# Row factors in fewer operations, three scale products moved to ScalarE, and a longer planned lag for eight spread matmuls

## The chip, the cores and the metric

The kernel runs on one core of a Trainium2 chip. The metric is device time in microseconds (us) for one launch, the median of several runs; lower is better. Engines are named as the profile names them: PE (TensorE matmul), PEld (TensorE weight load, which overlaps PE), DVE (VectorE), ACT (ScalarE), POOL (GpSimd), SP (SyncE, which here only issues DMAs). An engine with a small q behind it (SPq, POOLq) is that engine's queue issuing something.

## The reference

Three stages follow one another. Sizes: 2 batches, 8 heads, 768 steps, head size 40; so 1536 tokens of width 320.

```
# 1. gated linear attention, step by step (here done in chunks of 128 steps)
m_new = max(f + m, i);  f_stab = exp(f + m - m_new);  i_stab = exp(i - m_new)
C = f_stab * C + i_stab * outer(v, k);  n = f_stab * n + i_stab * k
y = sigmoid(o) * (C q) / max(|n.q|, 1)
# 2. dense mixture of 4 experts, every token through every expert
out = sum_e p[:, e] * (relu(x @ w1[e]) @ w2[e])        # w1: 320x1024, w2: 1024x320
# 3. routed mixture of 8 experts, capacity 384 tokens each
e = argmax(x @ w_gate);  y = gate * (relu(x @ w1[e]) @ w2[e])
```

The result is [1536, 320] in 32-bit floats.

## The kernel before

**Precision by splitting.** Matmuls run on 16-bit floats, and each 32-bit operand is split into a high and a low 16-bit part. Before a split, an operand is scaled by a power of two taken from its largest absolute value; `pow2_scale` makes that scale and its inverse with a few tiny DVE operations on exponent bits (lines 437 to 455). The inverses are multiplied back in later.

**Attention.** The 1536 tokens are 12 units (2 batches of 6 chunks of 128 steps), one tile of 128 tokens each. `front(u)` loads a unit, forms scales, decay and scores; `back(u)` applies the running state, updates it, forms the output row `y`, its scale `xs` and inverse `invx[:, u]`, splits it (`split_rows`) and transposes it by DMA into `xT`. Units 0 to 3 (`FP`) work in 32 bits and need no scales. Units 4 to 11 have four scales in `sm[:, 12:16]` and four inverses `iv` in `sm[:, 16:20]` (of q, k, v and the state). From them `front` forms three products on DVE: `iv1*iv2` (line 998), `iv1*iv2*iv0` (line 1000) and `iv0*iv3` (line 1004); the third scales the chunk decay `qd` on ACT (line 1008). They are read in `back`: `qd` by line 1224, the second by lines 1250 and 1255, the first by the state update of line 1291. Lines 1022 and 1028 split q and k, and line 1034 transposes them by DMA for the score matmuls of line 1114.

**Dense experts.** Weights are numbered k = 0 to 3 for the dense experts, 4 to 11 for the routed ones. Experts 0 and 1 run tile by tile between the attention units (`tile_ops`): layer 1 in two halves (PE line 645 into a PSUM bank, evacuated by ACT line 664 and DVE line 666), layer 2 (PE line 657), and then the accumulation `acc[t] += po * cf` on DVE (line 698; ACT line 692 for the first expert of a tile). The row factor `cf = pw[t, k] * invx[t]` is one number per token; line 686 forms it on POOL, one operation for each of 12 tiles and 4 experts, 48 in all. Experts 2 and 3 run afterwards over groups of four tiles (`group_ops`), and each tile that expert 3 finishes is routed at once (`route`).

**Weight preparation.** `w_max` finds a weight's largest magnitudes per partition (ACT line 528 or DVE line 533), reduces them over partitions on POOL into one `row` value (line 546), and spreads it over 128 partitions with a one-column PE matmul, the *spread* (line 552). The DVE operations of `pow2_scale` (lines 441 to 453) follow, then `w_conv` makes the high part (ACT line 590) and the low part (DVE line 595). Each of the two layers' weights passes through one raw buffer (`wraw`), in the order 0, 1, 2, 3, 8, 9, 10, 11, 4, 5, 6, 7: the next load (SP line 423) waits until the conversion before has read the buffer. Weights 8 to 11 are also stored to DRAM and fetched again later (`w_store`, `w_fetch`, line 503); after the last weight, 7, is converted, the copy of weight 8 is fetched into the raw buffers themselves, where layer 1 of an early window reads it.

**What sets the order.** Nothing issues in source order. `Sched` collects every operation with its engine, a cost in us, its reads and writes, then plays the whole program through (`starts`) and emits each engine's instructions in the planned order. `urgency` gives each operation a latest start, working back along the PE order given by the `at` keys; the most urgent ready one goes first. Spreads are different: `spot` puts a spread and the operation behind it into `now`, so PE takes a spread as soon as its planned ready time comes, ahead of all else; its key in `SPREAD_AT` only shapes the urgency of what leads to it. In planned time a spread in `late` becomes ready `SLACK` = 1.0 us after each operation it waits for (line 192). The last argument of `spot` (line 555) decides that: true for weights 1 to 3 and 8 to 11, false for 0 and 4 to 7. Engines execute their queues in order, so an instruction whose input is later than planned holds what is queued behind it. PE also gets filler matmuls (line 417) in planned gaps at the start.

Of the kernel before, what the change touches and what calls it, by code (L numbers as in the profile page):

```python
# [24 lines left out]
NT = B * NC  # L25
# [44 lines left out]
class Sched:  # L70
# [9 lines left out]
    def __init__(self):  # L80
        self.ops, self.last, self.readers, self.ahead = [], {}, {}, 0.0
        self.used, self.warm, self.filled = {}, None, 0.0
        self.spots, self.now, self.late, self.bank_of = [], set(), set(), {}

    def add(self, eng, us, fn, r=(), w=(), at=0.0):
        i = len(self.ops)
# [19 lines left out]
    def spot(self, fn, view, r, w, at, us):  # L106
        i = len(self.ops)
        self.add("PE", 0.07, lambda: fn(view(self.bank_of[i])), r, w, at)
        self.spots.append(i)
        self.now |= {i, i + 1}  # L110
        if us:
            self.late.add(i)
        return lambda: view(self.bank_of[i])

    @staticmethod
# [41 lines left out]
    def starts(self, lst):  # L157
        ops = self.ops
        n = len(ops)
        unit = [{"SCAT": "POOL", "TURN": "DMA", "ADMA": "ACT"}.get(op[0], op[0]) for op in ops]  # L160
        left = [len(op[3]) for op in ops]
        est, start = [0.0] * n, [0.0] * n
        users = [[] for _ in range(n)]
        free, ready, pipe, lanes, count = {}, {}, 0.0, [], 0
        for i, op in enumerate(ops):
            for d in op[3]:
                users[d].append(i)
            free[unit[i]] = self.BEGIN.get(unit[i], 0.0)
            if not left[i]:
                ready.setdefault(unit[i], []).append(i)  # L170
        while count < n:
            t, e = min((max(free[e], min(est[i] for i in c)), e) for e, c in ready.items() if c)
            i = min((i for i in ready[e] if est[i] <= t + self.HOLD[e]), key=lambda i: (i not in self.now, lst[i], i))
            ready[e].remove(i)
            if e == "DMA" and len(lanes) >= 8 and t < lanes[-8]:
                free[e] = lanes[-8]
                ready[e].append(i)
                continue
            start[i] = max(t, est[i])
            us = ops[i][1]  # L180
            count += 1
            free[e] = end = start[i] + us
            if e == "DMA":
                if ops[i][0] == "DMA":
                    free[e] = start[i] + 0.43
                    us = us if us >= 0.8 else 0.15
                    end = pipe = max(pipe, free[e]) + us
                else:
                    end = pipe = max(pipe, end)
                lanes.append(end + 1.7)  # L190
            for q in users[i]:
                est[q] = max(est[q], end + self.lag(ops[i][0], ops[q][0]) + self.care(ops[i][0], ops[q][0], end) + (SLACK if q in self.late else 0.0))
# [58 lines left out]
def xlstm_moe_kernel(ctx: ExitStack, tc: tile.TileContext, a, cap: int):  # L251
# [243 lines left out]
    def w_fetch(k, m, r=(), when=None, us=2.0):  # L495
# [17 lines left out]
    SPREAD_AT = {  # L513
        0: (SEQ["L", 0, 0] - 1.02, SEQ["M", 0, 0] - 2.02), 1: (SEQ["L", 1, 0] - 1.02, SEQ["M", 1, 0] - 1.02),
        2: (len(SEQ) - 0.1, at3 - 9.935), 3: (at3 - 5.61, at3 + 0.065), 8: (at3 + 0.39, at3 + 0.405),
        9: (at3 + 2.01, at3 + 2.03), 10: (at3 + 2.065, at3 + 2.095), 11: (at3 + 2.305, at3 + 2.39),
        4: (at3 + 4.005, at3 + 4.012), 5: (at3 + 4.054, at3 + 4.065), 6: (at3 + 4.19, at3 + 4.205), 7: (at3 + 4.405, at3 + 4.415),
    }

    def w_max(k, m):  # L520
        raw = wraw[m - 1].rearrange("p c f -> p (c f)")
        ks, n = ("wsm", k, m), 6 if m == 1 else 4
        w = raw.shape[1] // n
        am, t, mx = wsm[:, k, m - 1, 0:n], wsm[:, k, m - 1, 7:8], wsm[:, k, m - 1, 10:11]
        sc, iv = wscale(k, m)

        def part(i):
            nc.scalar.activation(  # L528
                out=junk[:, 0:w], in_=raw[:, i * w:(i + 1) * w], func=AF.Abs, accum_out=am[:, i:i + 1]
            )  # L530
# [23 lines left out]
        mx = sch.spot(  # L554
            spread, lambda b: bank[b][:, col:col + 1], [(ks, "row"), "const"], [(ks, "m")], SPREAD_AT[k][m - 1], 0 < k < 4 or k > 7
        )
        pow2_scale(sc, iv, t, mx, (CW1, CW2)[m - 1], [(ks, "m")], (ks, "i"), ks)
        if m == 2:
            vec(
                0.07, lambda: nc.vector.tensor_tensor(invp[:, k:k + 1], wscale(k, 1)[1], iv, ALU.mult),  # L560
                [(ks, "i"), (("wsm", k, 1), "i")], [("invp", k)],
            )
            if k < E1:
                vec(
                    0.13,
                    lambda: nc.vector.tensor_scalar(pw[:, :, k], probs[:, :, k], invp[:, k:k + 1], None, ALU.mult),
                    [("invp", k), "probs"], [("pw", k)],
                )
# [98 lines left out]
            [kp, kh] + ex, [kl],  # L667
        )

    begun = set()  # L670

    def l2_ops(k, t, wb, hh, hl, j, keys, at, extra=()):
        kp = ps_tile("o")
        po = bank[kp]
        for half in range(2):
# [262 lines left out]
    def front(u):  # L938
# [7 lines left out]
        pv2, qd = sm[:, 20:22], sm[:, 24:32]  # L946
        kr, kpb = ("raw", i3), ("pb", i3)
        va = raw[:, VA0:VA0 + HD]
        kr2 = ("raw2", i3)
# [37 lines left out]
        if not fp:  # L987
# [10 lines left out]
            vec(0.11, lambda: nc.vector.tensor_scalar(pv2[:, 0:1], iv1, iv2, None, ALU.mult), [("iv", u)], [("pv", u)])  # L998
            vec(
                0.09, lambda: nc.vector.tensor_scalar(pv2[:, 1:2], iv1, iv2, iv[:, 0:1], ALU.mult, ALU.mult),  # L1000
                [("iv", u)], [("pvq", u)],
            )
            vec(
                0.09, lambda: nc.vector.tensor_scalar(sm[:, 22:23], iv[:, 0:1], iv[:, 3:4], None, ALU.mult),
                [("iv", u)], [("iv03", u)],
            )
            act(
                0.22, lambda: nc.scalar.activation(out=qd, in_=qd3[:, b, c], func=AF.Copy, scale=sm[:, 22:23]),
                [("iv03", u), "qdec"], [("qd", u)],
            )  # L1010

# [167 lines left out]
    def back(u):  # L1179
# [4 lines left out]
        CC = Chr[i2]  # L1184
        kh, kl, kw = kdr[i2]
        sm = usm[:, u]
        pv2, qd, den = sm[:, 20:22], sm[:, 24:32], sm[:, 32:40]
# [56 lines left out]
        if fp and c > 0:  # L1244
            vec(0.45, lambda: nc.vector.tensor_tensor(O, pi, O, ALU.add), ["x2", ("O", i2)], [("O", i2)])
        elif fp:
            O, kO = pi, "x2"
        elif c > 0:
            vec(
                0.45, lambda: nc.vector.scalar_tensor_tensor(O, pi, pv2[:, 1:2], O, ALU.mult, ALU.add),  # L1250
                ["x2", ("O", i2), ("pvq", u)], [("O", i2)],
            )
        else:
            vec(
                0.45, lambda: nc.vector.tensor_scalar(O, pi, pv2[:, 1:2], None, ALU.mult),
                ["x2", ("pvq", u)], [("O", i2)],
            )
        if c < NC - 1:
# [27 lines left out]
            if fp:  # L1286
                vec(0.48, c_add, ["x3", kC], [kC])
            else:
                vec(
                    0.45,  # L1290
                    lambda: nc.vector.scalar_tensor_tensor(Cb, px[0:D], pv2[0:D, 0:1], Cb, ALU.mult, ALU.add),
                    ["x3", kC, ("pv", u)], [kC],
                )
            if fp and u + 1 not in FP:
# [727 lines left out]
```

## Time and profile before

| what | value |
|---|---|
| median of 3 runs | 496.33 us (495.67 to 498.98) |
| the profiled execution | 497.3 us, of which the span is 495.6 |
| PE busy | 477.2 us, 96% of the span |
| DVE, ACT, POOL busy | 338.7, 312.3, 131.6 us |
| PE's own waits | 11.2 us in 14 entries, longest 2.8 (at the start) |
| TensorE's granted clock | 0.989 of full speed over the span |

The profile comes from one execution of the program. The span runs from the first instruction to the last; the time of a run is a little longer. Busy shares are averages over stages with different limits, so each stage is read by itself. Where a line belongs to a helper (`pow2_scale`, `split_rows`, `evac_ops`), many operations share it, and the tile names tell them apart.

### The profile page before, as it was taken

The numbers are of one execution on the slowest core, as the hardware profiler recorded it, in microseconds if no ns is written. First come the engines' busy times: TensorE is split into PE (matmuls) and PEld (weight loads), VectorE is DVE, ScalarE is ACT, GpSimd is POOL, SyncE is SP. The second block draws the span as 40 slices with busy tenths as digits, with TensorE's granted clock in tenths as the row PEclk, the third lists the DMA queues.
The fourth block names the chain that finished last, engine by engine and source line by source line (L and its number), as shares of the span: only waits on it lengthen the run. The fifth ranks groups of instructions, "written<-read, shape, count | busy, mean of one in ns | idle before, by whom it ended". The sixth has DMA issues, their size and how long they took to land. (4 is left out here: it accounts for less than half of the span.)

```text
span 495.6 us, 13700 instructions
## 1 busy us (share of the span) xinstructions
PE 477.2 (96%) x5482; PEld 367.8 (74%) x5482; DVE 338.7 (68%) x971; ACT 312.3 (63%) x666; POOL 131.6 (27%) x243
## 2 busy tenths in 40 slices
PE   7999999999989899999999999999999999999994
PEld 6998989868878798887564746565565798878883
DVE  4599998799999834653968594879899882212120
ACT  1699989567687854956765668779789450322220
POOL 4533243665875410200010010000404011311111
PEclk9799999999999999999999999999999999999998
DMA  7879594264533795808695967727284536999300
GB/s 225 274 241 231 149 282 68 76 146 102 104 60 67 203 345 200 237 16 293 200 300 201 345 239 277 232 82 208 83 227 78 166 147 86 302 193 300 140 27 25
DMA packets 70772, 88.90 MB, mean 179 GB/s; under 512 B 48641, under 2 KB 56307, under 8 KB 70702
## 3 DMA queue, kind: packets, MB, share of 16 engines
q1 hardware_dynamic: 69502, 84.23, 59.9%
q0 software_dynamic: 1200, 3.73, 2.3%
q8 instruction: 45, 0.74, 0.6%
q14 instruction: 25, 0.20, 0.1%
HBM read 55.89 MB, written 21.70 MB: 157 GB/s over the span
## 5 line engine op out<-in xcount | busy, mean ns | idle before, releaser
L657 PEld LDWEIGHTS <-arena 128*128 128x128 f16 (+1 forms) x1416 | 136.1, 98 | 53.6 <-issue 2.5
L645 PEld LDWEIGHTS <-w 128*128 128x128 f16 x1792 | 97.0, 98 | 4.3 <-issue 2.8
L645 PE MATMUL ph<-xT,w 128*128 128x128 f16 (+3 forms) x1664 | 96.1, 218 | 1.2 <-DVE usm L443 0.9
L645 PEld LDWEIGHTS <-arena 128*128 128x128 f16 x960 | 64.2, 98 | 42.9 <-issue 1.5
L657 PE MATMUL po<-w,arena 128*128 128x320 f16 (+1 forms) x600 | 86.2, 299 | 1.3 <-DVE acc L698 1.3
L528 ACT ACTIVATE junk<-raw 128x512 bf16<-128x512 f32 (+1 forms) x105 | 69.5, 662 | 9.8 <-DMA raw<-in_moe_w_dram 8.2
L657 PE MATMUL po<-arena 128*128 128x320 f16 x504 | 71.3, 299 | 0.4 <-ACT arena L590 0.4
L666 DVE SCALAR_TENSOR_TENSOR arena<-ph,arena 128x512 f16<-128x512 f32 x80 | 54.5, 683 | 21.5 <-ACT arena L664 21.2
L645 PE MATMUL ph<-xT,arena 128*128 128x512 f16 (+4 forms) x512 | 66.7, 284 | 0.2 <-DMA xT<-disp 0.2
L590 ACT ACTIVATE w<-raw,wsm 128x640 f16<-128x640 f32 (+1 forms) x56 | 51.0, 959 | 18.2 <-DVE wsm L448 18.1
L664 ACT ACTIVATE arena<-ph 128x512 f16<-128x512 f32 x80 | 47.0, 587 | 24.2 <-PE ph L645 14.1
L595 DVE SCALAR_TENSOR_TENSOR w<-raw,wsm,w 128x640 f16<-128x640 f32 (+1 forms) x56 | 57.4, 1049 | 3.1 <-ACT w L590 3.0
L645 PE MATMUL x<-xT,arena 128*128 128x128 f16 (+4 forms) x448 | 52.2, 270 | 0.0
L546 POOL CROSS_LANE_REDUCE wsm<-wsm 128x1 f32<-128x6 f32 (+1 forms) x24 | 10.0, 418 | 103.0 <-ACT junk L528 71.1
L657 PE MATMUL x<-arena 128*128 128x320 f16 (+1 forms) x240 | 34.6, 300 | 0.4 <-ACT arena L1754 0.4
L595 DVE SCALAR_TENSOR_TENSOR arena<-raw,wsm,arena 128x640 f16<-128x640 f32 (+1 forms) x28 | 30.4, 1101 | 2.3 <-ACT arena L590 2.3
L590 ACT ACTIVATE arena<-raw,wsm 128x640 f16<-128x640 f32 (+1 forms) x28 | 25.5, 954 | 3.6 <-DVE wsm L448 3.6
L686 POOL TENSOR_TENSOR cfs<-pw,invx 128x1 f32<-128x1 f32 x48 | 17.0, 386 | 37.1 <-DVE invx L453 31.9
L698 DVE SCALAR_TENSOR_TENSOR acc<-po,cfs,acc 128x320 f32<-128x320 f32 x30 | 16.4, 546 | 14.6 <-PE po L657 7.5
L1765 POOL DMA_INDIRECT out_dram<-acc,usm x13 | 12.6, 973 | 46.1 <-ACT acc L1762 39.0
L1175 POOL TENSOR_TENSOR arena<-arena 128x512 f16<-128x512 f32 x16 | 20.6, 1305 | 12.6 <-ACT arena L1171 12.6
L1759 DVE SCALAR_TENSOR_TENSOR arena<-x,arena 128x512 f16<-128x512 f32 (+1 forms) x10 | 6.5, 652 | 24.4 <-ACT arena L1754 24.4
(235 smaller groups left out, 658.5 us busy)
## 6 DMA issues: line engine op xcount, KB each, us to landing
raw<-in_moe_w_dram SPq DMA_DIRECT2D x36, 512.0 KB
raw<-in_moe_w_dram SPq DMA_DIRECT2D x24, 640.0 KB
ws<-w SPq DMA_DIRECT2D x8, 768.0 KB
ws<-w SPq DMA_DIRECT2D x8, 640.0 KB
arena<-in_att_dram SPq DMA_DIRECT2D x8, 492.0 KB
disp<-zero SPq DMA_DIRECT2D x1, 3936.0 KB
arena<-ws SPq DMA_DIRECT2D x4, 768.0 KB
arena<-ws SPq DMA_DIRECT2D x4, 640.0 KB
```

Of the source, the lines that this page charges most:

```text
L528: nc.scalar.activation(out=junk[:, 0:w], in_=raw[:, i * w:(i + 1) * w], func=AF.Abs, accum_out=am[:, i:i + 1])
L546: 0.7 if k == 0 else 1.0, lambda: nc.gpsimd.tensor_reduce(row, am, AX.XYZWC, ALU.max), parts + ["wz"],
L590: lambda sl=sl: nc.scalar.activation(out=wh[:, sl], in_=raw[:, sl], func=AF.Copy, scale=sc),
L595: lambda sl=sl: nc.vector.scalar_tensor_tensor(wl[:, sl], raw[:, sl], sc, wh[:, sl], ALU.mult, ALU.subtract),
L645: nc.tensor.matmul(out=out, lhsT=wb[wi][:, c, f * 128:(f + 1) * 128], rhs=rhs(xc), start=(i == 0), stop=(i == LAST))
L657: nc.tensor.matmul(out=po[0:n, 0:DM], lhsT=hs[:, f, sl], rhs=ws[:, f, :], start=(f == 0 and i == 0), stop=(f == NF - 1 and i == 2),)
L664: act(0.52, lambda: nc.scalar.activation(out=hh, in_=ph, func=AF.Relu), [kp] + ex, [kh])
L666: 0.6, lambda: nc.vector.scalar_tensor_tensor(hl, ph, 0.0, hh, ALU.max, ALU.subtract),
L686: 0.26, lambda: nc.gpsimd.tensor_tensor(cf, pw[:, t, k:k + 1], invx[:, t:t + 1], ALU.mult),
L698: lambda: nc.vector.scalar_tensor_tensor(acc[:, t], po[:, 0:DM], cf, acc[:, t], ALU.mult, ALU.add),
L1175: 1.3, lambda j=j: nc.gpsimd.tensor_tensor(Wl[:, j::2], pb[:, j::2], Wh[:, j::2], ALU.subtract),
L1765: nc.gpsimd.indirect_dma_start(out=view_of(), out_offset=bass.IndirectOffsetOnAxis(ap=ix[0:n], axis=0), in_=acc[0:n, y], in_offset=None, b ...
```

## The change

Four edits. (1) Row factors: experts 2 and 3 get one POOL operation each over all 12 tiles; experts 0 and 1 get, for tiles 4 to 11, one ACT operation per tile that makes both factors; tiles 0 to 3 stay as they were. So 48 POOL operations become 10, and 8 ACT operations are new. (2) The three products per unit leave DVE: ACT makes `iv1*iv2`, and then, in one operation over two neighbouring columns, `iv3*iv0` and `iv1*iv2*iv0`. So 24 DVE operations go and 16 ACT operations come; `qd` now follows two ACT operations. (3) `late` holds a multiple of `SLACK`: 3 for the spreads of weights 8 to 11 (two each), 1 as before for weights 1 to 3. (4) The spread keys of weight 9 move by 0.02, two layer-1 pieces of a group.

```
-            self.late.add(i)
+            self.late[i] = us
...
-  ... + (SLACK if q in self.late else 0.0))
+  ... + (SLACK * self.late.get(q, 0)))
...
-        9: (at3 + 2.01, at3 + 2.03), 10: ...
+        9: (at3 + 2.03, at3 + 2.05), 10: ...
...
-  ... SPREAD_AT[k][m - 1], 0 < k < 4 or k > 7
+  ... SPREAD_AT[k][m - 1], 3 if k > 7 else int(0 < k < 4)
...
-        pool(
-            0.26, lambda: nc.gpsimd.tensor_tensor(cf, pw[:, t, k:k + 1], invx[:, t:t + 1], ALU.mult),
-            [("pw", k), ("xs", t, "inv")], [("cf", t, k)],
-        )
+        if (t, k) not in factored:
+            if k > 1:
+                js, ts, on_act = [k], range(NT), False
+            elif t < 4:
+                js, ts, on_act = [k], [t], False
+            else:
+                js, ts, on_act = [0, 1], [t], True
...
+            if on_act:
+                act(0.2, lambda: nc.scalar.activation(
+                        out=cfs[:, t, 0:2], in_=pw[:, t, 0:2], func=AF.Copy, scale=invx[:, t:t + 1]), r, w)
+            else:
+                tx = slice(ts[0], ts[-1] + 1)
+                pool(0.26, lambda: nc.gpsimd.tensor_tensor(cfs[:, tx, k], pw[:, tx, k], invx[:, tx], ALU.mult), r, w)
...
-            vec(0.11, lambda: nc.vector.tensor_scalar(pv2[:, 0:1], iv1, iv2, None, ALU.mult), ...)
-            vec(0.09, lambda: nc.vector.tensor_scalar(pv2[:, 1:2], iv1, iv2, iv[:, 0:1], ALU.mult, ALU.mult), ...)
-            vec(0.09, lambda: nc.vector.tensor_scalar(sm[:, 22:23], iv[:, 0:1], iv[:, 3:4], None, ALU.mult), ...)
+            act(0.2, lambda: nc.scalar.activation(out=pv, in_=iv1, func=AF.Copy, scale=iv2), [("iv", u)], [("pv", u)])
+            act(0.2, lambda: nc.scalar.activation(out=sm[:, 21:23], in_=sm[:, 19:21], func=AF.Copy, scale=iv[:, 0:1]),
+                [("iv", u), ("pv", u)], [("pvq", u), ("iv03", u)])
             act(
-                0.22, ... activation(out=qd, in_=qd3[:, b, c], func=AF.Copy, scale=sm[:, 22:23]),
+                0.22, ... activation(out=qd, in_=qd3[:, b, c], func=AF.Copy, scale=sm[:, 21:22]),
```

## Rows read from the trace of the kernel before

**Rows 1.** The page: busy time, share of the span and instructions of each engine.
```profile
PE 477.2 (96%) x5482; PEld 367.8 (74%) x5482; DVE 338.7 (68%) x971; ACT 312.3 (63%) x666; POOL 131.6 (27%) x243
```

**Rows 2.** Windows: length, then busy time of each engine, clock, DMA share, GB/s.
```profile
48.00:206.00 158.00, 152.69 (x2213) 131.22 (x2211) 133.22 (x343) 118.61 (x248) 70.43 (x123) 1.00 0.59 155
...
100.00:175.00 75.00, 69.69 (x1045) 58.72 (x1044) 70.16 (x175) 58.12 (x122) 45.49 (x59) 1.00 0.51 115
200.00:300.00 100.00, 99.01 (x769) 64.21 (x767) 70.14 (x130) 66.01 (x126) 8.24 (x22) 1.00 0.70 231
300.00:400.00 100.00, 99.57 (x719) 61.93 (x717) 81.93 (x317) 78.31 (x173) 15.90 (x31) 1.00 0.58 173
398.00:400.00 2.00, 2.00 (x43) 2.00 (x41) 1.45 (x9) 1.64 (x5) 0.00 (x0) 1.00 0.97 397
400.00:402.00 2.00, 2.00 (x43) 2.00 (x41) 1.88 (x18) 1.49 (x6) 0.00 (x0) 1.00 0.09 28
```

**Rows 3.** Waits of PE, by releaser: total, times, longest (us).
```profile
PE ph L417 <- POOL zero L759: 2.8, 1, 2.8
PE x L1114 <- DMA arena<-arena: 1.3, 2, 1.1
PE po L657 <- DVE acc L698: 1.3, 1, 1.3
PE x L1200 <- ACT arena L1171: 1.1, 1, 1.1
PE x L552 <- POOL wsm L546: 1.0, 1, 1.0
PE ph L645 <- DVE usm L443: 0.9, 1, 0.9
...
PE x L1268 <- POOL arena L1152: 0.4, 1, 0.4
```

**Rows 4.** Timeline, DVE around one unit's three products: start, us, instruction.
```profile
141.60 0.20 DVE L1004 TENSOR_SCALAR usm<-usm 128x1 f32<-128x1 f32 x1
141.72 0.27 DVE L1000 TENSOR_SCALAR usm<-usm 128x1 f32<-128x1 f32 x1
141.91 0.20 DVE L998 TENSOR_SCALAR usm<-usm 128x1 f32<-128x1 f32 x1
...
142.03 0.14 DVE L453 TENSOR_SCALAR invx<-usm 128x1 uint32<-128x1 uint32 x1
```

**Rows 5.** One line each: count, ns min/median/max, first and last start.
```profile
L1008 ACT ACTIVATE usm<-arena,usm x8: 292/295/307, 59.7 to 154.7; 128x8 f32<-128x8 f32 x8
L686 POOL TENSOR_TENSOR cfs<-pw,invx x48: 179/190/2827, 51.1 to 205.0; 128x1 f32<-128x1 f32 x48
L657 PE MATMUL po<-arena x504: 296/299/301, 244.9 to 470.4; 128*128 128x320 f16 x168
```

**Rows 6.** Waits of ACT between 48 and 206 us.
```profile
ACT arena L622 <- DVE usm L448: 3.9, 4, 1.8
```

**Rows 7.** Timeline, PE's wait at 118.29 and what DVE did before it.
```profile
117.03 0.54 DVE L1050 SCALAR_TENSOR_TENSOR arena<-arena,usm 128x328 f16<-128x328 f32 x1
...
117.56 0.67 DVE L666 SCALAR_TENSOR_TENSOR arena<-ph,arena 128x512 f16<-128x512 f32 x1
...
118.29 1.95 PE L645 MATMUL ph<-xT,w 128*128 128x128 f16 x32 [0.89 <-DVE usm L443]
```

**Rows 8.** Timeline, two maxima and the spreads behind them.
```profile
208.79 0.32 POOL L546 CROSS_LANE_REDUCE wsm<-wsm 128x1 f32<-128x6 f32 x1 [3.62 <-ACT junk L528]
...
212.53 0.17 PE L552 MATMUL x<-wsm,call 128*128 128x1 bf16 x1
...
288.12 1.30 POOL L546 CROSS_LANE_REDUCE wsm<-wsm 128x1 f32<-128x4 f32 x1 [7.52 <-DVE wsm L533]
...
289.47 0.16 PE L552 MATMUL x<-wsm,call 128*128 128x1 bf16 x1 [0.99 <-POOL wsm L546]
...
292.60 0.15 DVE L441 TENSOR_SCALAR wsm<-x 128x1 f32<-128x1 f32 x1
```

**Rows 9.** Waits of the SP queue between 200 and 402 us.
```profile
SPq L423 <- DVE w L595: 88.2, 24, 14.4
```

**Rows 10.** Timeline, the fetch into the raw buffers and its first reader.
```profile
393.02 1.51 SPq L503 DMA_DIRECT2D raw<-ws  x3
...
400.61 1.56 PE L645 MATMUL ph<-xT,raw 128*128 128x128 f16 x25
```

More of the change, by code (lines that the diff above doesn't have):

```diff
@@ L82, in __init__ @@
         self.used, self.warm, self.filled = {}, None, 0.0
-        self.spots, self.now, self.late, self.bank_of = [], set(), set(), {}
+        self.spots, self.now, self.late, self.bank_of = [], set(), {}, {}
     def add(self, eng, us, fn, r=(), w=(), at=0.0):
@@ L191, in starts @@
             for q in users[i]:
-                est[q] = max(est[q], end + self.lag(ops[i][0], ops[q][0]) + self.care(ops[i][0], ops[q][0], end) + (SLACK if q in self.late else 0.0))
+                est[q] = max(est[q], end + self.lag(ops[i][0], ops[q][0]) + self.care(ops[i][0], ops[q][0], end) + (SLACK * self.late.get(q, 0)))
                 left[q] -= 1
@@ L515, in xlstm_moe_kernel @@
         2: (len(SEQ) - 0.1, at3 - 9.935), 3: (at3 - 5.61, at3 + 0.065), 8: (at3 + 0.39, at3 + 0.405),
-        9: (at3 + 2.01, at3 + 2.03), 10: (at3 + 2.065, at3 + 2.095), 11: (at3 + 2.305, at3 + 2.39),
+        9: (at3 + 2.03, at3 + 2.05), 10: (at3 + 2.065, at3 + 2.095), 11: (at3 + 2.305, at3 + 2.39),
         4: (at3 + 4.005, at3 + 4.012), 5: (at3 + 4.054, at3 + 4.065), 6: (at3 + 4.19, at3 + 4.205), 7: (at3 + 4.405, at3 + 4.415),
@@ L554, in w_max @@
         mx = sch.spot(
-            spread, lambda b: bank[b][:, col:col + 1], [(ks, "row"), "const"], [(ks, "m")], SPREAD_AT[k][m - 1], 0 < k < 4 or k > 7
+            spread, lambda b: bank[b][:, col:col + 1], [(ks, "row"), "const"], [(ks, "m")], SPREAD_AT[k][m - 1], 3 if k > 7 else int(0 < k < 4)
         )
@@ L668, in evac_ops @@
         )
-    begun = set()
+    begun, factored = set(), set()
     def l2_ops(k, t, wb, hh, hl, j, keys, at, extra=()):
@@ L684, in l2_ops @@
         cf = cfs[:, t, k:k + 1]
-        pool(
-            0.26, lambda: nc.gpsimd.tensor_tensor(cf, pw[:, t, k:k + 1], invx[:, t:t + 1], ALU.mult),
-            [("pw", k), ("xs", t, "inv")], [("cf", t, k)],
-        )
+        if (t, k) not in factored:
[5 more added lines that the diff above has]
+                js, ts, on_act = [0, 1], [t], True
+            r = [("pw", x) for x in js] + [("xs", x, "inv") for x in ts]
+            w = [("cf", x, y) for x in ts for y in js]
+            factored.update((x, y) for x in ts for y in js)
+            if on_act:
+                act(
+                    0.2, lambda: nc.scalar.activation(
+                        out=cfs[:, t, 0:2], in_=pw[:, t, 0:2], func=AF.Copy, scale=invx[:, t:t + 1]
+                    ), r, w,
+                )
+            else:
+                tx = slice(ts[0], ts[-1] + 1)
+                pool(
+                    0.26, lambda: nc.gpsimd.tensor_tensor(cfs[:, tx, k], pw[:, tx, k], invx[:, tx], ALU.mult), r, w,
+                )
         if t not in begun:
@@ L945, in front @@
         am3, t4, sc, iv = (sm[:, 4 * x:4 * x + 4] for x in (0, 2, 3, 4))
-        pv2, qd = sm[:, 20:22], sm[:, 24:32]
+        pv, qd = sm[:, 20:21], sm[:, 24:32]
         kr, kpb = ("raw", i3), ("pb", i3)
@@ L997, in front @@
             iv1, iv2 = iv[:, 1:2], iv[:, 2:3]
[L998 to L1005, printed above, removed]
+            act(0.2, lambda: nc.scalar.activation(out=pv, in_=iv1, func=AF.Copy, scale=iv2), [("iv", u)], [("pv", u)])
+            act(
+                0.2, lambda: nc.scalar.activation(out=sm[:, 21:23], in_=sm[:, 19:21], func=AF.Copy, scale=iv[:, 0:1]),
+                [("iv", u), ("pv", u)], [("pvq", u), ("iv03", u)],
             )
             act(
-                0.22, lambda: nc.scalar.activation(out=qd, in_=qd3[:, b, c], func=AF.Copy, scale=sm[:, 22:23]),
+                0.22, lambda: nc.scalar.activation(out=qd, in_=qd3[:, b, c], func=AF.Copy, scale=sm[:, 21:22]),
                 [("iv03", u), "qdec"], [("qd", u)],
@@ L1186, in back @@
         sm = usm[:, u]
-        pv2, qd, den = sm[:, 20:22], sm[:, 24:32], sm[:, 32:40]
+        pv, pvq, qd, den = sm[:, 20:21], sm[:, 22:23], sm[:, 24:32], sm[:, 32:40]
         xam, xt, xs = sm[:, 40:41], sm[:, 41:42], sm[:, 42:43]
@@ L1249, in back @@
             vec(
-                0.45, lambda: nc.vector.scalar_tensor_tensor(O, pi, pv2[:, 1:2], O, ALU.mult, ALU.add),
+                0.45, lambda: nc.vector.scalar_tensor_tensor(O, pi, pvq, O, ALU.mult, ALU.add),
                 ["x2", ("O", i2), ("pvq", u)], [("O", i2)],
@@ L1254, in back @@
             vec(
-                0.45, lambda: nc.vector.tensor_scalar(O, pi, pv2[:, 1:2], None, ALU.mult),
+                0.45, lambda: nc.vector.tensor_scalar(O, pi, pvq, None, ALU.mult),
                 ["x2", ("pvq", u)], [("O", i2)],
@@ L1290, in back @@
                     0.45,
-                    lambda: nc.vector.scalar_tensor_tensor(Cb, px[0:D], pv2[0:D, 0:1], Cb, ALU.mult, ALU.add),
+                    lambda: nc.vector.scalar_tensor_tensor(Cb, px[0:D], pv[0:D], Cb, ALU.mult, ALU.add),
                     ["x3", kC, ("pv", u)], [kC],
```

## The prediction

> **What bounds the kernel now.** I read the page first: PE is busy for 477.2 of 495.6 us [rows 1]. No other engine comes near it, so the change can only be paid for in time in which PE stands still, and that is 18.4 us. Next I asked for windows, to see where that time lies. From 200 to 300 us PE idles 1.0 us and from 300 to 400 us 0.4 us; the stretch from 100 to 175 us holds 75 - 69.69 = 5.3 us [rows 2]. The rest is the start (2.8 us behind a memset [rows 3]) and the end, where nothing of the change lies. So 5.3 + 1.0 + 0.4 = 6.7 us is the most that the change can win without changing PE's own work.
>
> The third view, PE's waits, says who ended those stretches [rows 3]. Between 100 and 175 us they carry DVE's name or have DVE right behind them: DVE is busy for 70.2 of 75 us there, ACT for 58.1, POOL for 45.5 [rows 2]. The single wait of 200 to 300 us is a spread that came before its maximum, 0.99 us [rows 3, 8].
>
> **The change part by part.** The profiled execution took 497.3 us, 1.0 above the median of 496.33; the sum is made against 497.3 and the 1.0 is taken off at the end. Everything before about 51 us, where the first row factor and the first products stand [rows 4, 5], should keep its order, because the costs there are unchanged.
>
> *Row factors.* 38 of 48 POOL operations go. One takes 190 ns by the median, but up to 2827 when something holds it [rows 5]. PE hardly waits for POOL: 0.4 us for the low part of the decayed keys, and no row names a factor [rows 3]. So I take 0, with ends of -0.4 and 0. The merged operation of expert 2 now needs the inverses of all 12 tiles; the last old factor started at 205.0 us and expert 2's first layer-2 matmul at 244.9 [rows 5], so 40 us cover it. The eight new ACT operations I cost like the nearest row, a 128x8 product on ACT of 295 ns [rows 5]: 2.4 us, inside the 16.9 us that ACT idles between 100 and 175 us [rows 2]. They add a wait on ACT, for `invx`, and what is queued behind it there is PSUM evacuations, for which PE waits. ACT already waits four times, 3.9 us in all, for the same tile's scale [rows 6], made just before that inverse, so the new wait comes mostly on top of one that is there. If the cover goes, all 2.4 us fall on PE.
>
> *Scale products.* The three start at 141.60, 141.72 and 141.91 and the next instruction at 142.03 [rows 4]: 0.43 us of DVE's queue per unit, 3.4 us over 8 units (their durations overlap, so their sum would say too much). What is it worth on PE? At 118.29 PE waits 0.89 us for a bank that DVE line 666 empties from 117.56 to 118.23 [rows 7]; DVE ran without a pause since about 100 us, with one unit's three products and two of the next ahead of it: up to 0.7 us comes back. The waits of 1.1 (ACT line 1171), 1.1 (score matmuls behind a DMA) and 1.3 us (line 657) [rows 3] each have one unit's products upstream on DVE: 0.4 us each. Together -1.9 us. The ends are 0 (DVE then waits for something else) and -5.3 (all PE idle of this stretch [rows 2]); I take a value nearer to 0 because one wait regained moves PE on to the next. On ACT 16 operations come, 16 x 0.295 = 4.7 us. Planned well they fill idle time; planned badly a pair, 0.6 us, stands ahead of an evacuation or of line 1171. I take one such hit, +0.6; the ends are 0 and +7.1 (all 24 new ACT operations on PE). `qd` comes two ACT operations later, but only the next `back` reads it.
>
> Here a rule speaks against the edit. The trace shows ACT with 16.9 us idle and DVE with 4.8 in the same 75 us [rows 2], so the products move to the engine with room. The Trainium skill, "ScalarE: Activation LUTs", section "Rules for kernel authors", puts multiplications on VectorE, not on ScalarE; by it the edit would cost ACT time that DVE does more cheaply, and the sum would end above the time before. This trace does not bear that out for the engines' shares; the case has its own rival below.
>
> *Longer lag of the spreads.* From the end of its maximum to its spread I find 212.53 - 209.11 = 3.4 us for weight 8 but 289.47 - 289.42 = 0.05 us, after 0.99 us of waiting, for weight 11 [rows 8]: the real chain falls behind the plan. With 2 us more of planned lag PE would get there about 1 us after the maximum is ready: -0.9 us, ends -1.0 and 0. The price is that what follows (the four tiny DVE operations, the conversions, the next load into the same raw buffer) may come later. SP's loads already stand 88.2 us in total behind those conversions [rows 9], which is the chain that this lengthens, and what queues behind a waiting load on SP (stores, transposes of routed tiles) waits with it. In the trace the first DVE operation follows the last spread of weight 11 only 3.1 us later, at 292.60 [rows 8], so there is room in the chain itself; I take 0, with ends of 0 and +7.5 (worked out in the second rival). Weight 9's moved keys only lower its urgency by two layer-1 pieces: 0.
>
> *The new order.* New costs make the planner sort anew, and somewhere an input will be late that was in time. I take one new wait of the smallest size shown, +0.4 [rows 3]; the ends are 0 and two of the largest after the start, +2.6.
>
> Sum: 0 - 1.9 + 0.6 - 0.9 + 0.4 = -1.8 us; 497.3 - 1.8 = 495.5, less 1.0 gives **494.5 us**.
>
> **The rivals.**
>
> *Most of PE's idle time goes.* DVE relief ripples through 100 to 175 us. For it: DVE has only 4.8 us of slack there [rows 2], so 3.4 us less nearly doubles it. Against it: two of the waits hang on a DMA and on ACT [rows 3]. Time: 496.3 - 6.7 = 489.6.
>
> *Slower: the weight chain reaches PE.* Weights pass through one raw buffer per layer in series. If each of the four late weights is 2 us later and nothing absorbs it, the last conversion is 8 us later, and so is the fetch of weight 8's copy, issued from 393.02; DMA runs at 0.97 until 400 and falls to 0.09 after it, and PE reads that copy from 400.61 [rows 2, 10]. So the margin is some 0.5 us and PE would stand still for 8 - 0.5 = 7.5: 496.3 + 7.5 - 2.8 (the other gains) = 501.0. It decides from the point where that fetch is issued more than 0.5 us after 393.0. Against it: the room of 3 us behind a spread [rows 8], weights 4 to 7 that get no lag, and growing urgency towards the end.
>
> *ACT becomes the late engine.* The 24 new operations land ahead of evacuations: 496.3 + 7.1 - 0.9 = 502.5 at worst, half of it 498.9. For it: one PE wait already carries ACT's name [rows 3]. Against it: 39.4 us of ACT idle between 48 and 206 us [rows 2]. The rule of the Trainium skill cited above would lead here.
>
> *Nothing happens.* What DVE and the spreads give, another input takes: 495.3 to 497.3. For it: PE is at 99% in two of the three windows [rows 2]. In the same class is the case that the changed plan puts a spread no later than before.
>
> **How the numbers follow.** Forecast (491.4 to 495.3) 0.45; nothing 0.20; most idle gone 0.15; chain 0.13; ACT 0.07. One per cent is 5 us, so 491.4 and 501.3 are the marks, about what a measurement can tell from no change. Faster: 0.15 and 0.04 of the forecast's edge, 0.19. Slower: 0.07 of the chain (full price, with less of the gains) and 0.03 of ACT, 0.10. Same: 0.71. The range from 490.0 to 499.5 leaves out about 0.06 below and 0.11 above; -5.3 and -1.0 together are its lower end, half of the chain's or of ACT's price its upper.
>
> **What would show it.** In the profile after: lines 998 to 1004 absent from DVE and DVE's busy time between 100 and 175 us some 2 us lower (five units' products); PE's idle time there about 3.5 to 4 us instead of 5.3; two new ACT groups of near 0.3 us, 16 and 8 times, with no PE wait behind them; POOL's factor group at 10; no PE wait at line 552, and spreads of weights 8 to 11 some 2 us further behind their maxima; the fetch into the raw buffers still issued near 393 and no PE wait at its first reader. The forecast is wrong if PE's waits between 100 and 175 us stay at 5 us with the products gone, or if that fetch moves to 395 and beyond.

## The result and the profile after

The changed kernel took 500.46 us (median of 22 runs) against 497.31 us (22 runs) of the kernel before, measured together. The ratio is 1.007, with a 95% interval of 1.0045 to 1.0095: 3.5 us slower, where 1.8 us less had been forecast. Runs that a lower clock disturbed are left out of every ratio here.

The profiled execution took 500.87 us. Its page (columns as in [rows 1]) says first that TensorE has the same work, 476.8 us, in a span of 499.0 us instead of 495.6:

```profile
PE 476.8 (96%) x5482; PEld 367.4 (74%) x5482; DVE 338.6 (68%) x947; ACT 318.0 (64%) x690; POOL 115.2 (23%) x205
```

So PE idles 22.2 us, 3.8 more than before. VectorE (DVE) has 24 instructions fewer and is as busy as ever. The windows of the changed kernel, columns as in [rows 2], place the loss:

```profile
100.00:175.00 75.00, 68.16 (x1035) 57.30 (x1034) 71.11 (x160) 58.85 (x130) 34.67 (x40) 1.00 0.47 107
...
200.00:300.00 100.00, 99.69 (x784) 65.18 (x783) 70.02 (x129) 65.42 (x126) 7.38 (x20) 1.00 0.69 227
300.00:400.00 100.00, 96.80 (x654) 58.72 (x653) 80.55 (x305) 77.40 (x170) 15.02 (x31) 1.00 0.56 153
```

PE's idle time went from 5.3 to 6.8 us in the attention part, from 1.0 to 0.3 between 200 and 300 us, and from 0.4 to 3.2 between 300 and 400 us: +1.5 - 0.7 + 2.8 = +3.6 of the 3.8 us. PE's waits say who ended them (compare [rows 3]; lines 1184, 1213 and 1281 are 1171, 1200 and 1268 of before):

```profile
PE ph L645 <- DVE arena L666: 2.5, 4, 1.3
PE x L552 <- POOL wsm L546: 2.3, 1, 2.3
PE x L1213 <- ACT arena L1184: 1.9, 1, 1.9
PE x L1127 <- DMA arena<-arena: 1.5, 2, 0.9
...
PE x L1281 <- POOL arena L1165: 1.0, 1, 1.0
```

The new wait at line 552 is again a spread, but another one. In the timeline (start, us, instruction) weight 11's second spread, at 291.43, now comes 2.2 us after the end of its maximum and waits for nothing, against the 0.99 us of [rows 8]. Weight 4's second spread, at 311.23, which got no lag, waits 2.26 us:

```profile
288.94 0.33 POOL L546 CROSS_LANE_REDUCE wsm<-wsm 128x1 f32<-128x4 f32 x1 [6.89 <-DVE wsm L441]
...
291.43 0.17 PE L552 MATMUL x<-wsm,call 128*128 128x1 bf16 x1
...
295.32 0.14 DVE L441 TENSOR_SCALAR wsm<-x 128x1 f32<-128x1 f32 x1
...
309.09 0.74 ACT L528 ACTIVATE junk<-raw 128x640 bf16<-128x640 f32 x1 [1.61 <-DMA raw<-in_moe_w_dram]
...
310.85 0.33 POOL L546 CROSS_LANE_REDUCE wsm<-wsm 128x1 f32<-128x4 f32 x1 [5.62 <-ACT junk L528]
...
311.23 0.16 PE L552 MATMUL x<-wsm,call 128*128 128x1 bf16 x1 [2.26 <-POOL wsm L546]
...
398.37 2.23 SPq L503 DMA_DIRECT2D raw<-ws  x4
...
406.07 1.95 PE L645 MATMUL ph<-xT,raw 128*128 128x128 f16 x32
```

Read it backwards: the maximum waited for ACT's row maxima, and these for weight 4's load into a raw buffer, which is free only when the weight before it has been converted. In the kernel before, weight 4's second maximum stood here:

```profile
307.80 0.33 POOL L546 CROSS_LANE_REDUCE wsm<-wsm 128x1 f32<-128x4 f32 x1 [4.43 <-ACT junk L528]
```

So between the two profiles weight 11's maximum ends at almost the same time (289.42 and 289.27) and weight 4's ends 3.05 us later. The spread of weight 11 comes 2.1 us later behind its maximum, and the first DVE operation 3.9 us behind the spread instead of 3.1. The fetch that stood at 393.02 [rows 10] goes out at 398.37, 5.4 us later. But its first reader on PE comes 5.5 us later too, at 406.07 instead of 400.61, and does not wait: the distance from the fetch to its reader is 7.6 us before and 7.7 here. So the fetch's time says how late PE is at that point, and not by itself that the chain of weights holds PE up. Of the 5.5 us, 3.9 are idle time of PE up to there (13.7 against 9.8 us); the rest is work that the new order puts ahead of that reader.

In the attention part DVE lost what the products had given. This timeline shows a 128x320 product on DVE that takes 2.67 us where POOL's line 1188 runs beside it, and 6 us later the PE wait for the bank that DVE's line 666 empties, with no pause of DVE in between:

```profile
112.63 2.67 DVE L1339 SCALAR_TENSOR_TENSOR arena<-arena 128x320 f32<-128x320 f32 x1
112.68 2.27 POOL L1188 TENSOR_TENSOR arena<-arena 128x512 f16<-128x512 f32 x2
...
118.66 0.67 DVE L666 SCALAR_TENSOR_TENSOR arena<-ph,arena 128x512 f16<-128x512 f32 x1
...
119.39 0.83 PE L645 MATMUL ph<-xT,w 128*128 128x128 f16 x12 [1.34 <-DVE arena L666]
...
159.14 0.47 DVE L1339 SCALAR_TENSOR_TENSOR arena<-arena 128x320 f32<-128x320 f32 x1
```

The same line took 0.47 us at 159.14, with no POOL operation beside it. The edits of the work came out as costed, by the page's groups (busy, mean ns | idle before):

```profile
L704 POOL TENSOR_TENSOR cfs<-pw,invx 128x1 f32<-128x1 f32 (+1 forms) x10 | 3.1, 335 | 24.4 <-DVE invx L453 24.4
...
L1017 ACT ACTIVATE usm<-usm 128x2 f32<-128x2 f32 x8 | 2.4, 297 | 0.3
L1015 ACT ACTIVATE usm<-usm 128x1 f32<-128x1 f32 x8 | 2.3, 285 | 0.0
L697 ACT ACTIVATE cfs<-pw,invx 128x2 f32<-128x2 f32 x8 | 2.3, 282 | 0.0
```

### The profile page after: what moved, and what is told of

It reads as the page before. It is cut to its first block, busy times and chain, and to the rows that moved or that the text cites. A ratio compares the mean times of both kernels' runs of the same rounds, so it can differ in the third digit from the quotient of the medians.

```text
span 499.0 us, 13659 instructions
## 1 busy us (share of the span) xinstructions
PE 476.8 (96%) x5482; PEld 367.4 (74%) x5482; DVE 338.6 (68%) x947; ACT 318.0 (64%) x690; POOL 115.2 (23%) x205
## 5 line engine op out<-in xcount | busy, mean ns | idle before, releaser
L546 POOL CROSS_LANE_REDUCE wsm<-wsm 128x1 f32<-128x6 f32 (+1 forms) x24 | 8.8, 365 | 117.5 <-ACT junk L528 84.8
L1188 POOL TENSOR_TENSOR arena<-arena 128x512 f16<-128x512 f32 x16 | 19.5, 1235 | 15.1 <-ACT arena L1184 15.0
L1109 POOL TENSOR_SCALAR_AFFINE_SELECT arena<-arena 128x512 f32<-128x512 f32 x24 | 18.0, 763 | 19.6 <-ACT arena L1097 12.4
```

The source lines that it names most:

```text
L1109: lambda j=j: nc.gpsimd.affine_select(out=pb[:, j::2], in_=pb[:, j::2], pattern=[[0, H // 2], [1, 128]], compare_op=ALU.is_ge, fill=0.0, b ...
L1188: 1.3, lambda j=j: nc.gpsimd.tensor_tensor(Wl[:, j::2], pb[:, j::2], Wh[:, j::2], ALU.subtract),
```

## The experiments

The theories set against each other: that the new order costs the time (O), and in it either the new sort of the planner (S) or the longer lag and the chain of weights behind it (L, C); that the work moved to ACT costs it (W); that the prediction's terms hold (P).

### The work in the order of before (e4_old_order)

The planner gets the old entries with their old costs, and the new operations are issued from the old places, so PE and SP have the order of before; the lag is the old one.

```
-            vec(0.11, lambda: nc.vector.tensor_scalar(pv2[:, 0:1], iv1, iv2, None, ALU.mult), ...)
+            vec(0.11, products, [("iv", u)], [("pv", u)])
...
-            0.26, lambda: nc.gpsimd.tensor_tensor(cf, pw[:, t, k:k + 1], invx[:, t:t + 1], ALU.mult),
+        pool(0.26, factor, [("pw", k), ("xs", t, "inv")], [("cf", t, k)])
```

> Edits 1 and 2 as work, but in the order of the kernel before: PE's and SP's instructions stand exactly as before, the new ACT operations stand where the replaced ones were planned, no lag. Theory O: the saved DVE time shows: PE's idle time between 100 and 175 us falls from 5.3 to about 3.5 to 4.5, 0.5 to 2 us faster than before. Rival W: slower than before by 1 to 3 us, since the ACT operations are the same. Rival P: 1.3 us faster, as the prediction's terms for edits 1 and 2 sum to.

Measured: 495.02 us, ratio 0.9966 (0.9936 to 0.9995), faster by 1.7 us. Its page and windows:

```profile
PE 476.9 (97%) x5482; PEld 367.9 (75%) x5482; DVE 333.1 (68%) x947; ACT 317.6 (64%) x690; POOL 120.4 (24%) x205
```

```profile
100.00:175.00 75.00, 72.03 (x1072) 60.79 (x1071) 67.09 (x162) 62.96 (x143) 38.67 (x42) 1.00 0.54 128
...
300.00:400.00 100.00, 98.16 (x718) 60.95 (x717) 81.42 (x318) 76.70 (x167) 15.84 (x31) 1.00 0.56 163
```

PE idles 3.0 us in the attention part instead of 5.3, and DVE's busy time there fell to 67.1. ACT has the same added operations as the changed kernel (317.6 against 318.0 us), so W falls. The same 947 DVE instructions take 5.5 us less than in the changed kernel (333.1 against 338.6). Two lines hold that difference and more. Of this kernel, then of the changed one:

```profile
L1042 DVE SCALAR_TENSOR_TENSOR arena<-arena,usm 128x320 f16<-128x320 f32 x16 | 8.6, 547 | 1.8 <-ACT arena L1036 1.8
...
L1340 DVE SCALAR_TENSOR_TENSOR arena<-arena 128x320 f32<-128x320 f32 x11 | 6.5, 590 | 0.1
```

```profile
L1041 DVE SCALAR_TENSOR_TENSOR arena<-arena,usm 128x320 f16<-128x320 f32 x16 | 11.8, 753 | 1.5 <-ACT arena L1035 1.5
L1339 DVE SCALAR_TENSOR_TENSOR arena<-arena 128x320 f32<-128x320 f32 x11 | 10.0, 910 | 0.1
```

These two lines follow the order, and not the execution: they sum to 15.1 us here and in e8_best below, to 17.1 us in the kernel before, e7_moved and e11_two_moved, and to 21.8 us in the changed kernel, e5_no_lag and e12_after_moved. PE's idle time in the attention part is 3.0 us in both of the first group, 4.8 to 5.4 in the second and 6.5 to 6.8 in the third. The two don't always go together: e1_lag has 17.1 and 3.5, e6_old_work 20.0 and 7.4.

### The old work in the new order (e6_old_work)

```
-            act(0.2, lambda: nc.scalar.activation(out=pv, in_=iv1, func=AF.Copy, scale=iv2), ...)
+            act(0.2, lambda: nc.vector.tensor_scalar(pv, iv1, iv2, None, ALU.mult), [("iv", u)], [("pv", u)])
...
+                for x in ts:
+                    for y in js:
+                        nc.gpsimd.tensor_tensor(cfs[:, x, y:y + 1], pw[:, x, y:y + 1], invx[:, x:x + 1], ALU.mult)
```

> The changed kernel's order on PE and SP, lag included, but the old operations: products on DVE, 48 factors on POOL. Theory O: the new work is worth 1 to 2 us here too, so this is 1 to 2 us slower than the changed kernel, about 4 to 6 us slower than before. Rival W (the new ACT operations cost): faster than the changed kernel, 496 to 498.

Measured: 501.5 us, 1.0068 (1.0025 to 1.0112), as slow as the changed kernel with none of its new operations, where the expectation had it 1 to 2 us slower: in the new order the new work is worth nothing that these runs can tell. PE idles 7.4 us in the attention part, 2.1 more than before with the same work:

```profile
100.00:175.00 75.00, 67.59 (x1002) 56.83 (x1001) 70.78 (x177) 52.45 (x107) 38.91 (x53) 0.98 0.46 101
```

The wait for ACT's line 1184 (1181 here) is 2.0 us long, 1.9 in the changed kernel and 1.1 before: it belongs to the order, not to ACT's new work. Weight 4's second spread waits 1.04 us here. Part of this execution's time is clock: from 140 to 150 us the mean granted clock was 0.83, between its two levels, where it is 1.00 (2.4 GHz) in the changed kernel.

### Parts of the change, each planned anew (e1_lag, e2_products, e3_factors, e5_no_lag)

The lag alone (edits 3 and 4 on the kernel before):

```
-  ... SPREAD_AT[k][m - 1], 0 < k < 4 or k > 7
+  ... SPREAD_AT[k][m - 1], 3 if k > 7 else int(0 < k < 4)
```

> Only edits 3 and 4 (the lag of 3 for the eight spreads and weight 9's keys); row factors and products as before. Theory O (the time was lost to the lag and to the new order, not to the new operations): the wait of 0.99 us at the spread of weight 11 goes, and weight 4's second spread, which has no lag, waits about 2.3 us in its place, as in the profile after; PE's idle time between 100 and 175 us stays near 5.3; 1 to 2 us above the time before. Rival W (the new ACT operations cost the time): the lag is neutral, within 0.5 us of the time before. Rival P (my prediction's step): 0.9 us faster.

Measured: 502.19 us, 1.0127 (1.0084 to 1.017). Here the attention part is better than before (3.5 us idle), and the waits that are new lie behind 300 us, at three spreads without the longer lag, the second ones of weights 4, 6 and 7:

```profile
309.25 0.16 PE L552 MATMUL x<-wsm,call 128*128 128x1 bf16 x1 [0.72 <-POOL wsm L546]
...
358.28 0.16 PE L552 MATMUL x<-wsm,call 128*128 128x1 bf16 x1 [0.88 <-POOL wsm L546]
...
388.63 0.16 PE L552 MATMUL ph<-wsm,call 128*128 128x1 bf16 x1 [1.22 <-POOL wsm L546]
```

They add up to 2.8 us; the ratio makes 6.3. The profiled execution took 499.99 us, 2 us less than the median, so these rows can't hold all of the loss.

The products alone (edit 2, the third block of the change's diff):

> Only edit 2 (the three products as two ACT operations), planned anew. Theory O: DVE's queue loses 3 ops a unit, but the new order puts other DVE operations beside POOL's and in front of evacuations, so PE's idle time between 100 and 175 us is not lower than 5.3 and the time is 0 to 2 us above before. Rival W: 1 to 3 us slower, with PE waits that carry ACT's name right behind a product operation. Rival P: about 1.3 us faster, PE idle there about 4.

Measured: 498.41 us, 1.0017 (0.9982 to 1.0051), with 7.2 us of idle time in the attention part. The factors alone (edit 1):

> Only edit 1 (48 POOL factors as 10 POOL and 8 ACT operations), planned anew. Theory O: the work is worth nothing on PE, the new order moves PE's waits by up to 2 us either way. Rival W: slower by about 1 us, waits behind ACT's factor operations. Rival P: the same time as before within 0.5 us.

Measured: 500.64 us, 1.0088 (1.0063 to 1.0113), idle 4.3 us there, with waits of 1.06 and 1.00 us at the second spreads of weights 11 and 4. The whole change without the longer lag:

```
-  ... SPREAD_AT[k][m - 1], 3 if k > 7 else int(0 < k < 4)
+  ... SPREAD_AT[k][m - 1], int(0 < k < 4 or k > 7)
```

> The changed kernel with the lag of weights 8 to 11 back at 1 (edits 1, 2 and 4 stay, planned anew). Theory O (the new order costs, and so does the lag): if the lag's cost adds to the rest, some 4 to 6 us faster than the changed kernel, near 495; if each new sort is a draw of its own, anywhere from 495 to 501, with its own waits in other places. Rival L (the lag alone is the loss): as fast as the old order with the new work, 494 to 496.

Measured: 504.45 us, 1.0144 (1.0093 to 1.0195): idle 6.7 us in the attention part, and 1.11 and 1.57 us of waiting at the spreads of weights 11 and 4. This one speaks against a simple story in which the lag is all of the loss. Beside e4_old_order, which has the same work and the same lag (only edit 4 is added here), it shows what the sort alone can cost: 1.0144 against 0.9966. Each of these four kernels has an order of its own, and their ratios don't add: 1.0127 and 1.0144 are the lag alone and everything but the lag, and together they make 1.007. They can't price a part.

### The lag without a new sort (e7_moved)

The eight spreads of weights 8 to 11 are issued 2 us later in the finished plan of the kernel before:

```
+        for i in self.spots:
+            if i in self.moved:
+                start[i] += 2.0
+                for q in succ[i]:
+                    start[q] = max(start[q], start[i] + 0.27)
...
+        if k > 7:
+            sch.moved.add(sch.spots[-1])
```

> The kernel before with only the eight spreads of weights 8 to 11 emitted 2 us later in PE's order, without a new sort; 30 lines of PE's order differ. It parts the lag itself from the sort that it causes. Theory C (the chain of weights is late by the lag): the wait at weight 11's spread goes, weight 4's second spread waits 1 to 2 us, the fetch into the raw buffers is issued 1 to 3 us later than 393, and the time is 1 to 4 us above before. Theory S (the 6 us of the lag alone come from the new sort): within 1 us of before, or 1 us faster.

Measured: 500.63 us, 1.0057 (1.0025 to 1.009). The fetch goes out 3.6 us later than in [rows 10] (line 509 here), and its reader comes 3.6 us later too. PE's waits (lines 6 or 8 higher than in [rows 3]) have one of 1.2 us at weight 4's second spread, and 2.5 us for the banks that DVE empties:

```profile
396.59 1.52 SPq L509 DMA_DIRECT2D raw<-ws  x3
```

```profile
PE ph L653 <- DVE arena L674: 2.5, 3, 1.5
...
PE x L558 <- POOL wsm L552: 1.2, 1, 1.2
```

The longest of them stands right behind weight 8's second spread (219.87), and 0.79 us right behind weight 11's (294.13). DVE's first operation on the spread stood 2.31 us for it, with the evacuation that PE needs queued behind:

```profile
220.10 0.16 DVE L447 TENSOR_SCALAR wsm<-x 128x1 f32<-128x1 f32 x1 [2.31 <-PE x L558]
...
221.55 1.95 PE L653 MATMUL ph<-xT,w 128*128 128x128 f16 x32 [1.51 <-DVE arena L674]
```

In the kernel before, DVE stood 2.05 us for the same spread, but the spread (at 216.06) came further ahead of the matmul that needs the bank, and PE didn't wait. So the lag costs by itself, with the old work and the old sort, and in this profile 2.3 of the 3.5 us of new waits come from DVE held behind a moved spread, 1.2 from the chain of weights. This price doesn't carry over to the changed kernel as it stands: there the planner placed DVE's operations with the lag in view, and PE idles 0.3 us between 200 and 300 us, against 2.5 here.

### One more spread moved in the changed kernel (e12_after_moved)

```
+        if (k, m) == (4, 2):
+            sch.moved.add(sch.spots[-1])
```

> The changed kernel with its work, order and lag; only weight 4's second spread, at which TensorE now waits 2.3 us, is emitted 2 us later in the finished plan. Theory that the lag only moved the wait from one spread to the next, and that this wait costs its length: ratio 1.002 to 1.004 to the kernel before, no wait at a spread in 300 to 325 us. Rival, that the chain of weights is the limit: the 2 us come back as waits behind the fetch into the raw buffers (issued at 398.4, then 400 or later), ratio 1.006 to 1.009, as the changed kernel's 1.007. Rival, that the sort in the attention part carries the whole loss: 1.005 to 1.007 with TensorE's idle time between 100 and 175 us still near 6.8 us.

Measured: 497.63 us, 1.0024 (0.9987 to 1.0061). The wait is gone: the spread at 311.81 comes 3 us after its maximum, and PE idles 0.5 us between 300 and 400 us instead of 3.2, while the attention part keeps 6.5. Timeline and windows:

```profile
308.52 0.33 POOL L552 CROSS_LANE_REDUCE wsm<-wsm 128x1 f32<-128x4 f32 x1 [4.84 <-ACT junk L534]
...
311.81 0.17 PE L558 MATMUL x<-wsm,call 128*128 128x1 bf16 x1
...
395.25 2.23 SPq L509 DMA_DIRECT2D raw<-ws  x4
```

```profile
100.00:175.00 75.00, 68.46 (x1039) 57.57 (x1038) 70.34 (x160) 59.15 (x131) 34.25 (x40) 1.00 0.49 107
...
300.00:400.00 100.00, 99.49 (x711) 61.70 (x710) 81.39 (x315) 77.87 (x172) 16.06 (x31) 1.00 0.57 158
```

The ratio fell by 0.0046, 2.3 us, which is about the length of the wait. But the two ratios come from different sets of runs, and their intervals share 1.0045 to 1.0061. And the two profiles differ ahead of the moved spread, where the two kernels have the same instructions in the same order. The first load of weight 10's second matrix goes out at the same time in both, and DVE's row maxima that wait for it start 1.4 us apart. Of the changed kernel, then of this one:

```profile
256.11 0.33 SPq L423 DMA_DIRECT2D raw<-in_moe_w_dram  x1
...
262.59 1.54 DVE L533 TENSOR_REDUCE wsm<-raw 128x1 f32<-128x640 f32 x2 [2.52 <-DMA raw<-in_moe_w_dram]
```

```profile
256.10 0.33 SPq L429 DMA_DIRECT2D raw<-in_moe_w_dram  x1
...
261.16 1.55 DVE L539 TENSOR_REDUCE wsm<-raw 128x1 f32<-128x640 f32 x2 [0.80 <-DMA raw<-in_moe_w_dram]
```

With weight 11's loads the difference grows to 2.0 us: its second spread comes 4.4 us behind its maximum here and 3.9 in e6_old_work, which has the same order, but 2.2 in the changed kernel's profile. In this execution weight 4's maximum ends at 308.85, and an unmoved spread would have waited some 0.2 us (an estimate: PE stood at it at 308.97 in the changed kernel, and runs 0.26 us earlier here). So most of the 2.26 us belongs to one execution's late loads, and this run does not price that wait. The fetch, at 395.25, is 3.1 us earlier than in the changed kernel, and so is its reader.

### The faster version (e8_best), and its parts

The work in the old order, as in e4_old_order, and only the two spreads that wait there moved by 2 us:

```
+        if (k, m) in ((11, 2), (4, 2)):
+            sch.moved.add(sch.spots[-1])
```

> The old order with the new work, and only the two spreads that wait there (the second ones of weights 11 and 4, 0.72 and 0.65 us) emitted 2 us later, without a new sort. Theory O: the two waits go, 0.5 to 1.4 us faster than the old order with the new work, about 494 or 2 to 3 us below the kernel before. Theory C: the waits reappear at the spreads of weights 5 to 7 and nothing is won.

Measured: 494.78 us, 0.9929 (0.9889 to 0.997), 3.5 us faster than the kernel before. No PE wait is left at a spread, and the fetch went out at 391.7:

```profile
100.00:175.00 75.00, 72.04 (x1068) 60.55 (x1066) 68.50 (x164) 62.73 (x142) 39.66 (x43) 1.00 0.54 121
...
300.00:400.00 100.00, 99.51 (x735) 62.15 (x733) 82.58 (x327) 78.48 (x173) 15.80 (x31) 1.00 0.57 171
```

Three further kernels take it apart, each in the order of before: the products alone, the factors alone, and the two moved spreads with the old work. Their edits are the halves of the two diffs above.

> The order of the kernel before on TensorE, the same transfers and the same lag; only the three scale products per unit go from VectorE (24 operations less) to ScalarE (16 more, each put where the first or second of the old products stood in the plan). With both parts of the work changed in this order the ratio was 0.9966 and TensorE idled 3.0 us between 100 and 175 us instead of 5.3. Theory that the products carry that gain (VectorE was busy for 70.2 of these 75 us, POOL for 45.5): ratio 0.996 to 0.9975, TensorE idle 3.0 to 3.6 us there, VectorE busy near 67.5 us. Rival, that the row factors carry it (38 POOL operations less, so fewer stretches in which POOL and VectorE hold each other up): 0.999 to 1.001 and idle time near 5 us. As predicted, the products alone would be worth -1.3 us, 0.9974.

> The order of the kernel before on TensorE, the same lag; only the row factors change (10 POOL operations and 8 on ScalarE instead of 48 on POOL), each issued where the last or first of its old ones stood. Theory that the products carry the gain of the work: ratio 0.999 to 1.001, TensorE idle between 100 and 175 us 4.8 to 5.3 us. Rival, that the factors carry it: 0.9965 to 0.998, idle time 3 to 4 us. As predicted, the factors are worth 0 (-0.4 to 0 us, and up to +2.4 on ScalarE): 0.999 to 1.0.

> The kernel before with its old work and order; only two of its spreads, the second of weight 11 and the second of weight 4, are emitted 2 us later in the written plan (the two that stood waiting at TensorE once the work had changed). Prediction's term for the longer lag: -0.9 us where the spread waits and 0 for the chain, so 0.998 to 0.9985, with no wait of TensorE at a spread. Rival, that the chain of weights pays it back as when all eight late spreads were moved (1.0057): 1.0 to 1.003, with the fetch into the raw buffers at 394 or later instead of 393.0. If the work and the two moved spreads add, this one makes up 0.9929 / 0.9966 = 0.9963.

Measured: 1.0004 (0.9966 to 1.0043), 1.001 (0.9974 to 1.0046) and 1.0001 (0.9964 to 1.0037). None can be told from 1. The first two can't be told from the fraction expected of them either; the third leaves room for the prediction's 0.998, and 0.9963, which would have made up the whole, lies just outside its interval. The three ratios multiplied make 1.0015, not 0.9929: inconclusive. The factors leave 4.5 us of PE idle time in the attention part; the moved spreads, with the old work, 4.75 against the 5.3 of before, so one execution differs from another by about 0.5 us there. (The products' windows are not used: TensorE's granted clock was 0.968 over that span, against 0.989 before.) Which part gives what stays open.

## Why the prediction was wrong

**The bound was right.** PE's idle time decided, and the changed kernel's loss is idle time, in the stretches that were named.

**Row factors and products: right in size, where the order stays.** The sum had 0 for the factors and -1.9 + 0.6 = -1.3 us for the products; in the order of before both together give -1.7 us (0.0005 to 0.0064 of the time). The halves alone showed nothing of it (1.0004 and 1.001), so its division stays open. The new ACT operations took 282 to 297 ns, against the 295 taken from [rows 5], and no PE wait stands behind them.

**"The new order: +0.4" failed.** With the same work and the same lag the new sort came out at 1.0144 (e5_no_lag) and the old one at 0.9966 (e4_old_order). With the same work the attention part idles 6.8 us in the new order and 3.0 in the old: +3.8 us; with the old work it is 7.4 against 5.3, +2.1. The end of +2.6 that the prediction gave covers only the second. Other executions bear the sizes out: 6.7 us in e5_no_lag and 6.5 in e12_after_moved, 3.0 in e8_best. The step treated a new sort as one late input. It changes, among much else, which of DVE's and POOL's operations meet: as I read the traces, the products' relief of DVE was lost to DVE's two-input operations that were held beside POOL's (15.1 us of them against 21.8). The prediction's own sign, waits that stay at 5 us with the products gone, is what came.

In this kernel a 128x320 operation of DVE took 2.67 us with a POOL operation beside it, and 0.47 us elsewhere. The Trainium skill, "SBUF — State Buffer", section "SBUF: two separate sides", says that a VectorE operation with two SBUF inputs and a GpSimd operation that reads SBUF exclude each other for a whole instruction; the trace agrees, with that row. No run took the POOL operation away by itself, so that this overlap makes the 1.34 us wait at 119.39 is read from the timeline, not shown by an edit.

**"Longer lag: -0.9" held in place, "chain: 0" did not.** Weight 11's wait of 0.99 us went. The 0 for the chain was argued from 3.1 us of room between the spread and the first DVE operation behind it [rows 8]. That room was not slack. DVE's operation is placed behind the spread in the plan and moved with it, to 295.32, 3.9 us behind 291.43. In the changed kernel's profile the delay went through conversion, raw buffer and load into the next weight's maximum, and PE waited 2.26 us at the first spread without a longer lag. Its size is not a fixed price: the same order gave 1.04 us in e6_old_work, and some 2 us of the 2.26 came with loads that arrived late in that one execution. That the lag isn't free is shown by e7_moved (1.0057, no new sort), though there most of it was paid at DVE, a path that the prediction did not have.

**The rival "the weight chain reaches PE"** gave 501.0, and 500.46 came, by luck. Its point of decision was passed, for the fetch went out 5.4 us later, but the sign was badly chosen: the fetch and its reader move together (7.6 to 7.7 us apart in every kernel with the order of before or of the changed kernel), so a late PE passes it as well as a late chain. PE never waits at that fetch's reader. It had waited at weight 4's spread, 87 us before that fetch goes out, and for 2.3 us, not 7.5. And 1.5 us more are the sort's, in the attention part, which the rival did not have.

**ACT as the late engine** is excluded by e4_old_order, which has all of ACT's new work and is faster.

**The account**, in PE's idle time against the kernel before: the work -2.3 us and the new order +3.8 in the attention part, weight 11's spread -0.7 (by its window), the stretch with weight 4's spread +2.8. Together +3.6, against 3.5 by the ratio and -1.8 forecast. This is one execution of each kernel: the numbers of the attention part came again in other executions, that of weight 4's stretch did not (1.5 us of idle time between 300 and 400 us in e6_old_work, in the same order, against 3.2). So the cause that is shown is the order, and not the work; what share of the 3.5 us in the median is the lag's is not shown.

**Open:** how much of weight 4's wait is the lag's. Without it, but in another sort, that spread waits 1.57 us (e5_no_lag), and with the old order 0.65 (e4_old_order), because PE then arrives earlier. And e5_no_lag is slower than the change itself, so in a new sort the lag may even have paid; no run holds that sort fixed and takes the lag out.

## What to carry to other kernels

Where a planner sorts the work, a changed cost is two changes: price the new operations in the old order first, for the kernels sorted anew here came out at ratios from 1.002 to 1.014, in no relation to the size of their edit. In a serial chain, look at where a delayed link's successors stand in their queues: eight links moved by 2 us cost 1.0057 here, and two moved links nothing that could be told (1.0001), with the last spread at 382.3 us, 382.2 before. A point of decision should be a distance between two events, not the time of one, which moves with all that lies ahead of it. And room between two instructions is slack only if the second has a fixed place: see who sets its start.

## What the runs showed of the hardware that was not expected

The same 128x320 DVE instruction took 0.47 to 2.67 us, by what POOL did beside it. A load that went out at 256.1 us, with the same instructions in the same order ahead of it, was awaited by DVE until 262.59 us in one execution and until 261.16 in another. TensorE's clock added to a loss: in the kernel with the lag alone PE was busy 4.03 of 5 us from 420 to 425 us, and in the next 5 us, with 4.38 busy, the mean granted clock was 0.70, between the levels of 1.2 and 2.4 GHz, before it came back. These windows have the columns of [rows 2]:

```profile
420.00:425.00 5.00, 4.03 (x124) 3.85 (x122) 0.08 (x2) 0.23 (x1) 0.39 (x2) 1.00 0.69 74
425.00:430.00 5.00, 4.38 (x46) 3.11 (x46) 1.73 (x6) 2.28 (x6) 3.00 (x3) 0.70 0.95 268
430.00:435.00 5.00, 4.75 (x114) 4.33 (x113) 0.00 (x0) 0.55 (x2) 0.93 (x1) 0.95 1.01 387
```
